# Batch 0's first chain and batch 1's v, regrouped: V spread beside k.z, A in halves, v loaded whole, stores and tails in other places of the queue

## The chip, the cores and the metric

The kernel runs on one core of a Trainium2 chip. The metric is device time in microseconds (us), the median of several executions; lower is better. The chip's engines run beside each other: TensorE (PE, with its weight loads PEld), VectorE (DVE), ScalarE (ACT), GpSimd (POOL) and the queue engine SyncE (SP). DMAs are issued from SP's, POOL's or ACT's queue. Each engine works through its own instructions in the program's order and waits at semaphores for the others.

## The reference, cut to what matters

Eight batches, eight heads, a sequence of 576, a head width of 64. A cosine-weighted linear attention feeds a mixer with a low-rank product over the sequence and an MLP over the channels:

```python
# q, k, v: (8, 8, 576, 64)
phi(x) = concat([relu(x) * cos(theta), relu(x) * sin(theta)])   # theta = pi/2 * pos / 576
kv  = einsum('bhsf,bhsd->bhfd', phi(k), v);  z = phi(k).sum(over s)
x   = einsum('bhsf,bhfd->bhsd', phi(q), kv) / (einsum('bhsf,bhf->bhs', phi(q), z) + 1e-6)
x   -> (8, 576, 512)                                # heads side by side
u   = x + ((x^T @ U) @ V)^T                         # U: 576x32, V: 32x576
out = u + relu(u @ w_ch1) @ w_ch2                   # w_ch1: 512x2048, w_ch2: 2048x512
```

## The kernel before

A sequence of 576 is cut into four chunks of 128 rows (c = 0 to 3) and a tail of 64 (c = 4). The rows lie so that a partition holds consecutive rows of the sequence: a load of q, k or v has an "odd" DMA (`load_odd`, four rows for every odd partition) and an "even" one (`load_even`, five rows for every even partition, the fifth being the tail). From batch 2 on the tail has a DMA of its own (`load_tail`) beside the two of `load_main`. The staging buffers `qst`, `kst` and `vst` exist once each; a batch's load waits until the batch before has been read out of them.

The program is an order written out by hand (manual schedule). Each engine's instructions stand in the order in which the Python code emits them. Buffers come from pools; a PSUM tile takes the next buffer of its tag (X: one pair of banks; T: one; o: two; g: three) and waits until the last user of that buffer is done.

**The head (batch 0).** PE runs warm-up matmuls on zeros (`keep_warm`) while q, k and v of batch 0 land. DVE and ACT make phi(q) (`q_prep`), PE transposes it, DVE and ACT copy it out; then comes phi(k) (`k_prep`), and for each chunk eight one-column matmuls add up z (L842), with one warm-up matmul after each chunk. `cast_uv` on POOL prepares U and V. Then `first_chain(0)`: v is cast in blocks, `kv_unit` makes kv for four heads at a time (heads 0 to 3, then 4 to 7), `den_mm` and `recip` make the reciprocal of the denominator, `xh_mm` makes x of four heads of one chunk, and `xh_norm` (L728, DVE) multiplies it by the reciprocal. `spread_v` (L223, L226) spreads V over the partitions, in the middle of the second group of x; ACT casts it. `a_mm` makes A = x^T U for the columns 0 to 255, later for 256 to 511; `open_mm` transposes x into a PSUM tile `uT_ps` for one quarter d of the channels, `uTd_mm` adds V^T A to it, and `uTd_evac` casts it to `uT`.

**The mixer.** `g1_main(b, j)` multiplies uT by column block j (of 16) of w_ch1: four matmuls of 512 columns, then a relu on ACT (`hid`). w_ch1 and w_ch2 are loaded by POOL in four DMAs each (`w1_load(n)` holds j = 4n to 4n+3). `g2_part(pr, cc, part)` multiplies hid by a quarter of w_ch2's rows; after the fourth part DVE adds u (`o_sb`), and a DMA stores it. Batches go in pairs pr = 0 to 3; cc = 0 to 3 are the first batch's chunks, cc = 4 is both tails, and 5 to 8 are the second's chunks.

**Slots.** The main part is a list of slots: one `g1_main`, one `g1_tail` or one `g2_part` each, four matmuls of 512 columns (0.86 us) as a rule. Pair 0 has the slots 0 to 15 (g1 of batch 0), 16 to 31 (the early g2 parts of cc 0 to 3), 32 to 47 (g1 of batch 1), 48 to 51 (tails), 52 to 71 (the rest of g2); pair 1 begins at slot 72 with 32 slots of g1, 4 of tails and then 36 of g2. After slot i come the thunks put at i: attention steps of the next batch, loads, DMA transposes. For batch 1 these are `q_prep` and `qtr_unit` (slots 0 to 5), `k_prep` (6, 7, 9, 10, 12), `v_prep` of heads 0 to 3 at 11 and of heads 4 to 7 at 13 (both on DVE), `kv_unit` of heads 0 to 3 at 14 and of 4 to 7 at 15, x from 16 on. Batches 2 to 7 follow `attention_plan`.

```python
for i in range(2):
    at(11 + 2 * i, lambda c=c, i=i: v_prep(1, 4 * i, 4 * i + 4, (c,), (V_,)))
for hg in range(2):
    at(14 + hg, lambda hg=hg: kv_unit(1, hg, "T", 1))
```

Batch 1's v is loaded by four DMAs, odd and even rows of heads 0 to 3 and then of heads 4 to 7. In pair 0 the stores of cc 0 to 4 and 8 go out on POOL as soon as they are ready, those of cc 5 and 6 on SP at slot 65 (`late`), that of cc 7 on SP at once.

## Time and profile before

| | |
|---|---|
| three runs, median (lowest to highest) | 309.15 us (309.09 to 309.82) |
| profiled execution | 309.09 us |
| its span (first to last instruction) | 307.3 us |
| PE busy | 300.0 us (98%) in 2304 matmuls |
| DVE, ACT, POOL busy | 149.2, 139.5, 51.6 us |
| granted TensorE clock, mean | 0.997 |
| HBM read and written | 36.86 and 9.44 MB |

What lies between the span and the execution's time (309.09 - 307.3 = 1.8 us) is the start and the end of the program around its instructions. In the page a row names line, engine, operation, out<-in, its shape and count, and then busy time, mean duration in ns, and the idle time before it with what ended it. Timeline rows have start, length, engine and line; a bracket at the end tells how long the engine had been idle and what it waited for. Consecutive matmuls overlap in these rows: one of 512 columns lasts 379 ns, but the next begins 216 ns after it. A DMA's row (SPq) is its issue alone; its landing is told apart.

### The profile page before, as it was taken

What the parts mean: (1) busy time and instruction counts of PE and PEld (TensorE: products, weight loads), DVE (VectorE), ACT (ScalarE), POOL (GpSimd) and SP (SyncE); (2) the same over time, 40 slices, a digit from 0 to 9 for tenths busy, and PEclk for the clock granted to TensorE, in tenths of its full rate; (3) what the DMA queues carried; (4) which work ended last, traced back from release to release, by engine and by line L of the source; (5) the groups of instructions that cost most, each with busy time, mean ns of one, the idle gap of its engine ahead of it and who ended that gap; (6) DMA issues with size and microseconds to landing.
All of it is one profiled execution on the core that took longest, in us unless ns stands there. A gap on an engine that the chain in (4) does not pass through costs nothing.

```text
span 307.3 us, 5726 instructions
## 1 busy us (share of the span) xinstructions
PE 300.0 (98%) x2304; PEld 157.3 (51%) x2329; DVE 149.2 (49%) x354; ACT 139.5 (45%) x237; POOL 51.6 (17%) x91
## 2 busy tenths in 40 slices
PE   8989999999999999999999999999999999999995
PEld 3676464448445444664455444574455444474443
DVE  4988565873876592166336591146327510001111
ACT  2935921265860566589100466579200366630000
POOL 8411200350120016004221400004221000000000
PEclk9999999999999999999999999999999999999998
DMA  6999999999999969992989579922971140001221
GB/s 213 352 260 255 245 194 233 229 329 221 293 215 203 300 147 264 243 250 78 212 213 344 164 124 218 275 64 79 182 161 46 58 85 0 0 2 68 78 95 68
DMA packets 90445, 54.26 MB, mean 177 GB/s; under 512 B 58484, under 2 KB 87444, under 8 KB 90420
## 3 DMA queue, kind: packets, MB, share of 16 engines
q1 hardware_dynamic: 83956, 43.20, 60.0%
q0 software_dynamic: 6320, 10.64, 14.1%
q8 instruction: 18, 0.29, 0.4%
q10 hardware_dynamic: 144, 0.07, 0.1%
q14 instruction: 7, 0.06, 0.1%
HBM read 36.86 MB, written 9.44 MB: 151 GB/s over the span
## 4 chain that ended last, share of the span: by engine, by line
PE 94%; DMA 2%; DVE 1%; issue 1%; ACT 0%; ACTq 0%; DVEq 0%
PE o_ps L585 40%; PE g_ps L531 36%; PE gt_ps L551 5%; PE kv_ps L299 3%; PE x_ps L390 2%; DMA qst<-in_q_dram 2%; PE va_ps L435 2%; PE t_ps L328 1%; PE a_ps L415 1%; PE t_ps L316 1%; PE w_ps L193 1%; PE z_ps L842 0%; PE va_ps L438 0%; PE x_ps L904 0%; DVE x_bf L728 0%
## 5 line engine op out<-in xcount | busy, mean ns | idle before, releaser
L540 ACT ACTIVATE hid<-g_ps 128x512 bf16<-128x512 f32 x128 | 76.1, 598 | 106.9 <-PE g_ps L531 106.8
L585 PE MATMUL o_ps<-w_bf,hid 128*128 128x512 bf16 (+2 forms) x509 | 117.4, 372 | 0.9
L531 PE MATMUL g_ps<-uT,w_bf 128*128 128x512 bf16 x512 | 116.8, 379 | 0.0
L531 PEld LDWEIGHTS <-w_bf 128*128 128x128 bf16 x512 | 48.7, 98 | 56.9 <-issue 1.7
L585 PEld LDWEIGHTS <-hid 128*128 128x128 bf16 x528 | 48.5, 98 | 51.9 <-issue 1.1
L595 DVE TENSOR_TENSOR o_sb<-u_bf,o_ps 128x512 f32<-128x512 bf16 (+2 forms) x33 | 22.1, 669 | 57.0 <-PE o_ps L585 55.9
L608 POOL DMA_DIRECT2D out_dram<-o_sb x21 | 13.2, 630 | 125.5 <-DVE o_sb L595 56.3
L110 POOL CAST v_ext<-vst 128x512 bf16<-128x512 f32 (+1 forms) x26 | 20.6, 815 | 27.5 <-PE g_ps L531 14.8
L110 DVE CAST kv<-kv_ps 128x260 bf16<-128x260 f32 (+1 forms) x15 | 6.4, 429 | 37.2 <-PE kv_ps L299 37.2
L442 DVE TENSOR_TENSOR u_bf<-x_bf,va_ps 128x512 bf16<-128x512 bf16 x24 | 16.5, 687 | 10.1 <-PE va_ps L435 10.1
L363 DVE TENSOR_SCALAR rec<-x_ps 128x8 f32<-128x8 f32 (+2 forms) x39 | 6.3, 162 | 20.1 <-PE x_ps L390 19.4
L551 PE MATMUL gt_ps<-uT_tl,w_bf 128*128 128x128 bf16 x256 | 15.9, 219 | 0.0
L400 DVE TENSOR_TENSOR x_bf<-x_ps,rec 128x512 bf16<-128x512 f32 x22 | 15.2, 691 | 0.8
L551 PEld LDWEIGHTS <-w_bf 128*128 128x128 bf16 x256 | 14.7, 98 | 0.9
L585 PE MATMUL o_ps<-w_bf,hid_tl 128*128 128x512 bf16 x61 | 14.6, 379 | 0.2
L193 PE MATMUL w_ps<-zero 128*128 128x512 bf16 x36 | 11.9, 445 | 1.3 <-DVE zero L119 1.2
L299 PEld LDWEIGHTS <-k_p 128*128 128x128 bf16 x256 | 11.2, 97 | 3.2
L558 ACT ACTIVATE hid_tl<-gt_ps 128x512 bf16<-128x512 f32 x16 | 9.6, 597 | 6.6 <-PE gt_ps L551 6.6
L258 ACT ACTIVATE k_p<-kst,sinw 128x512 bf16<-128x512 f32 x17 | 11.9, 714 | 0.0
L299 PE MATMUL kv_ps<-v_ext,k_p 128*128 128x65 bf16 (+1 forms) x256 | 11.8, 193 | 0.0
L260 DVE TENSOR_SCALAR q_p<-qst,cosw 128x512 bf16<-128x512 f32 x21 | 9.8, 479 | 3.1 <-DMA qst<-in_q_dram 3.1
L390 PEld LDWEIGHTS <-q_pT 128*128 128x128 bf16 x176 | 8.5, 98 | 4.7
(137 smaller groups left out, 245.9 us busy)
## 6 DMA issues: line engine op xcount, KB each, us to landing
qst<-in_q_dram SPq DMA_DIRECT2D x14, 512.0 KB, 5.8
kst<-in_k_dram SPq DMA_DIRECT2D x14, 512.0 KB, 7.5
vst<-in_v_dram SPq DMA_DIRECT2D x12, 512.0 KB, 8.4
out_dram<-o_sb POOLq DMA_DIRECT2D x21, 256.0 KB, 4.7
w_bf<-in_moe_w_ch_dram POOLq DMA_DIRECT2D x8, 512.0 KB, 12.7
out_dram<-o_sb SPq DMA_DIRECT2D x10, 256.0 KB, 2.4
qst<-in_q_dram SPq DMA_DIRECT2D x2, 640.0 KB, 6.5
kst<-in_k_dram SPq DMA_DIRECT2D x2, 640.0 KB
```

The costliest lines, as they stand in the source:

```text
L110: eng.tensor_copy(out=o, in_=i)
L193: nc.tensor.matmul(out=w_ps, lhsT=zero[:, 0:P], rhs=zero, start=True, stop=True)
L299: nc.tensor.matmul(out=acc[:, i, :], lhsT=k_of(b, c, h), rhs=v_tl[:, h, 0:n] if c == 4 and b < 2 else vx[:, c, h, 0:n], start=(c == 0), st ...
L390: nc.tensor.matmul(out=acc[:, g, i * E : i * E + E], lhsT=qT_of(b, c, h), rhs=kv_sb[b][:, h, :], start=True, stop=True,)
L400: nc.vector.tensor_tensor(out=x_of(b, c, rows).rearrange("p (g i d) -> p g i d", g=2, d=D), in0=view[:, :, :, 0:D], in1=rec[rows].unsqueez ...
L442: nc.vector.tensor_tensor(out=u_bf[b][:, c, :] if c < 4 else u_tl[b // 2], in0=x_of(b, c), in1=va, op=ALU.add,)
L531: nc.tensor.matmul(out=g_ps.rearrange("p (c t) -> p c t", c=4), lhsT=w1_bf[:, d, j * P : j * P + P], rhs=uT[b][:, :, d, :], start=(d == 0) ...
L540: nc.scalar.activation(out=hid[b][:, j, :], in_=g_ps, func=AF.Relu, bias=0.0, scale=1.0)
L551: nc.tensor.matmul(out=g_ps[:, jj, :], lhsT=w1_bf[:, d, j * P : j * P + P], rhs=uT_tl[pr][:, d, :], start=(d == 0), stop=(d == 3),)
L585: nc.tensor.matmul(out=o[:, cols], lhsT=lhs[:, j, c * P : c * P + P], rhs=w2_bf[:, j, cols], start=(j == 0), stop=(j == NJ - 1),)
L595: nc.vector.tensor_tensor(out=o_sb[:, cols], in0=u[:, cols], in1=o[:, cols], op=ALU.add)
L608: eng.dma_start(out=out[b].rearrange("(m k) n -> m k n", k=9)[:, c : c + 6 : 5, cols], in_=o_sb[:, cols],)
```

## The change

- The odd rows of batch 0's q are issued from ACT's queue, not SP's.
- V's spread: its two matmuls stand after chunk 2 of the z loop, in two tiles of tag g, and replace the warm-up matmul there. The other warm-up matmuls of that loop write the second bank of z's own tile, and the last one a tile of tag o. ACT's casts of V stand before kv's.
- First chain: x of heads 0 to 3 of one chunk (ORD[3]) is normalised by four ACT instructions in place of one on DVE. x of heads 4 to 7 uses the three g buffers and the pair X. A's first half, the four quarters of uT and the first g matmuls are in a new order: quarters 0 and 1 of uT in tags T and o, 2 and 3 in X and T; the first three j get their matmuls for d = 0 together (`g_half`), then those for d = 1.
- Batch 1's v is loaded by two DMAs, odd and even rows of all heads.
- Pair 0's stores of cc 1 to 4 go to SP at slot 92; `o_sb` has eight buffers in place of four. cc 5 to 8 and cc 0 stay as they were.
- Batch 2's loads: q's main rows at slot 15, its tail at 26, then k's and v's tail and main rows at 26. Its `q_prep` takes the tail last.

```diff
-    load_odd(qst, q, 0)
+    load_odd(qst, q, 0, eng=A_)
...
-    def spread_v(eng):
-        v_ps = ps.tile([P, 2, 512], FP32, tag="X", bufs=1, name="v_ps")
...
+    def spread_v():
+        for cs in (slice(0, 512), slice(512, S)):
+            t = ps.tile([P, 512], FP32, tag="g", bufs=3, name="v_ps")
+            n = cs.stop - cs.start
+            nc.tensor.matmul(
+                out=t[:, 0:n], lhsT=four, rhs=V_nat[:, cs], start=True, stop=True
+            )
+            v_ps.append(t)
+    def spread_evac(eng):
+        cast(eng, V_bf, v_ps[0].rearrange("r (c p) -> r c p", c=4))
+        cast(eng, V_tl, v_ps[1][:, 0:TS])
...
+    def g_half(b, d, js):
+        for j in js:
+            if d == 0:
+                g_open[b, j] = ps.tile([P, 512], FP32, tag="g", bufs=3, name="g_ps")
+            nc.tensor.matmul(
+                out=g_open[b, j].rearrange("p (c t) -> p c t", c=4),
+                lhsT=w1_bf[:, d, j * P : j * P + P],
+                rhs=uT[b][:, :, d, :],
+                start=(d == 0),
+                stop=False,
+            )
...
-        o_sb = pool.tile([P, DM], FP32, tag="o_sb", bufs=4, name="o_sb")
+        o_sb = pool.tile([P, DM], FP32, tag="o_sb", bufs=8, name="o_sb")
...
+        if pr == 0 and 0 < cc < 8:
+            eng = nc.sync
...
-        if pr == 0 and 5 <= cc < 8:
-            eng = nc.sync
-            if cc < 7:
-                late.append(store)
-                return
+        if pr == 0 and 0 < cc < 7:
+            late.setdefault(92 if cc < 5 else 65, []).append(store)
+            return
         store()
...
-            put(f_at + n, q_prep, c, (q_eng, q_eng))
+            put(f_at + ((n - 1) % 5 if b == 2 else n), q_prep, c, (q_eng, q_eng))
...
         v_prep(b, 4, 8, (4,), (A_,))
+        spread_evac(A_)
...
         x0.append(xh_mm(b, ORD[4], 0, *O2))
+        for i in range(4):
+            nc.scalar.activation(
+                out=x_of(b, ORD[3])[:, i * D : i * D + D], in_=x0[3][:, i, :],
+                func=AF.Copy, bias=0.0, scale=rec[0][:, ORD[3], i : i + 1],
+            )
+        xh_norm(b, ORD[2], 0, rec[0], x0[2])
+        recip(rec[1], d[1])
+        xh_norm(b, ORD[4], 0, rec[0], x0[4])
...
-        x1 = [xh_mm(b, c, 4, *t) for c, t in zip(ORD, (T1, G3))]
-        spread_v(A_)
-        x1 += [xh_mm(b, c, 4, *t) for c, t in zip(ORD[2:], (G3, G3, O2))]
-        for n in range(5):
-            xh_norm(b, ORD[n], 4, rec[1], x1[n])
+        x1 = [xh_mm(b, c, 4, *G3) for c in ORD[0:3]]
+        x34 = ps.tile([P, 2, 512], FP32, tag="X", bufs=1, name="x34_ps")
+        for i in range(2):
+            x1.append(x34[:, i, 0:256].rearrange("p (i d) -> p i d", d=D))
+            xh_mm(b, ORD[3 + i], 4, acc=x1[-1])
...
+        for i, (tag, bufs) in enumerate((T1, O2)):
+            uT_ps[b, i] = ps.tile([P, 4, P], FP32, tag=tag, bufs=bufs, name="uT_ps")
+            open_mm(b, i, uT_ps[b, i], range(4))
         for i in range(2):
-            open_mm(b, i, t[i], range(4))
-        uTd_mm(b, 0)
+            uTd_mm(b, i)
         uTd_evac(b, 0, A_)
-        uTd_mm(b, 1)
+        for n in range(5):
+            xh_norm(b, ORD[n], 4, rec[1], x1[n])
         uTd_evac(b, 1, V_)
         a_mm(b, a_ps, 256, 512, range(5))
         cast(A_, A_of(b)[:, 256:512], a_ps[:, 256:512])
...
+        js = range(3)
+        g_half(b, 0, js)
+        for i in (2, 3):
+            uTd_mm(b, i)
+        g_half(b, 1, js)
+        uTd_evac(b, 2, V_)
+        uTd_evac(b, 3, A_)
...
-    for h0 in (0, 4):
-        load_odd(vst, v, 1, h0, h0 + 4)
-        load_even(vst, v, 1, h0, h0 + 4)
+    load_odd(vst, v, 1)
+    load_even(vst, v, 1)
...
-        if n == 1:
-            put(15, lambda: load_tail(kst, k, 2))
-            put(26, lambda: load_main(kst, k, 2))
-        else:
-            put((15, 0, 26)[n], t)
+        if n == 0:
+            put(15, lambda: load_main(qst, q, 2))
+            put(26, lambda: load_tail(qst, q, 2))
+        else:
+            put(26, t)
```

More of the change, by code (lines that the diff above doesn't have):

```diff
@@ L71, in load_even, with load_odd @@
         )
-    def load_odd(dst, src, b, h0=0, h1=H):
-        nc.sync.dma_start(
+    def load_odd(dst, src, b, h0=0, h1=H, eng=nc.sync):
+        eng.dma_start(
             out=dst[1:P:2, h0:h1, 0:4].rearrange("m h c d -> m h (c d)"),
@@ L219, in cast_uv @@
             cast(G_, U_bf[tail(i), 4 + i, :], stU[tail(i), 4, :])
-    def spread_v(eng):
-        v_ps = ps.tile([P, 2, 512], FP32, tag="X", bufs=1, name="v_ps")
-        nc.tensor.matmul(
-            out=v_ps[:, 0, :], lhsT=four, rhs=V_nat[:, 0:512], start=True, stop=True
-        )
-        nc.tensor.matmul(
-            out=v_ps[:, 1, 0:TS], lhsT=four, rhs=V_nat[:, 512:S], start=True, stop=True
-        )
-        cast(eng, V_bf, v_ps[:, 0, :].rearrange("r (c p) -> r c p", c=4))
-        cast(eng, V_tl, v_ps[:, 1, 0:TS])
+    v_ps = []
+    def spread_v():
[9 more added lines that the diff above has]
+        cast(eng, V_tl, v_ps[1][:, 0:TS])
     k_p, q_p, q_pT, kv_sb, x_bf = {}, {}, {}, {}, {}
@@ L563 @@
     o_ps = {}
-    late = []
+    late = {}
     def g2_part(pr, cc, part):
@@ L598, in g2_part @@
         eng = nc.gpsimd if pr < NPAIR - 1 else nc.scalar if part == 3 and last else nc.sync
-        if cc == 4:
-            for i in range(2):
-                eng.dma_start(
-                    out=out[2 * pr + i].rearrange("(m k) n -> m k n", k=9)[:, 4, :],
-                    in_=o_sb[i * TS : i * TS + TS, :],
-                )
-            return
-        def store():
+        if pr == 0 and 0 < cc < 8:
+            eng = nc.sync
+        def store():
+            if cc == 4:
+                for i in range(2):
+                    eng.dma_start(
+                        out=out[2 * pr + i].rearrange("(m k) n -> m k n", k=9)[:, 4, :],
+                        in_=o_sb[i * TS : i * TS + TS, :],
+                    )
+                return
             eng.dma_start(
@@ L611, in store @@
             )
-        if pr == 0 and 5 <= cc < 8:
-            eng = nc.sync
-            if cc < 7:
-                late.append(store)
-                return
+        if pr == 0 and 0 < cc < 7:
+            late.setdefault(92 if cc < 5 else 65, []).append(store)
+            return
         store()
@@ L714, in den_mm, with xh_mm @@
                 )
-    def xh_mm(b, c, h0, tag, bufs):
-        acc = ps.tile([P, 4, D], FP32, tag=tag, bufs=bufs, name="xh_ps")
+    def xh_mm(b, c, h0, tag=None, bufs=None, acc=None):
+        if acc is None:
+            acc = ps.tile([P, 4, D], FP32, tag=tag, bufs=bufs, name="xh_ps")
         for h in range(h0, h0 + 4):
@@ L788, in first_chain @@
         x0.append(xh_mm(b, ORD[4], 0, *O2))
+        for i in range(4):
+            nc.scalar.activation(
+                out=x_of(b, ORD[3])[:, i * D : i * D + D], in_=x0[3][:, i, :],
+                func=AF.Copy, bias=0.0, scale=rec[0][:, ORD[3], i : i + 1],
+            )
+        xh_norm(b, ORD[2], 0, rec[0], x0[2])
+        recip(rec[1], d[1])
+        xh_norm(b, ORD[4], 0, rec[0], x0[4])
         for _ in range(2):
@@ L792, in first_chain @@
             )
-        for n in range(2, 5):
-            xh_norm(b, ORD[n], 0, rec[0], x0[n])
-            if n == 3:
-                recip(rec[1], d[1])
-        x1 = [xh_mm(b, c, 4, *t) for c, t in zip(ORD, (T1, G3))]
-        spread_v(A_)
-        x1 += [xh_mm(b, c, 4, *t) for c, t in zip(ORD[2:], (G3, G3, O2))]
-        for n in range(5):
-            xh_norm(b, ORD[n], 4, rec[1], x1[n])
+        x1 = [xh_mm(b, c, 4, *G3) for c in ORD[0:3]]
+        x34 = ps.tile([P, 2, 512], FP32, tag="X", bufs=1, name="x34_ps")
+        for i in range(2):
+            x1.append(x34[:, i, 0:256].rearrange("p (i d) -> p i d", d=D))
+            xh_mm(b, ORD[3 + i], 4, acc=x1[-1])
         uT_alloc(b)
-        u03 = ps.tile([P, 2, 512], FP32, tag="X", bufs=1, name="u03")
-        t = [u03[:, i, :].rearrange("p (c t) -> p c t", c=4) for i in range(2)]
         a_ps = ps.tile([P, DM], FP32, tag="o", bufs=2, name="a_ps")
@@ L807, in first_chain @@
         cast(A_, A_of(b)[:, 0:256], a_ps[:, 0:256])
-        for tag, bufs in (T1, O2):
-            t.insert(-1, ps.tile([P, 4, P], FP32, tag=tag, bufs=bufs, name="uT_ps"))
-        for i in range(4):
-            uT_ps[b, i] = t[i]
+        for i, (tag, bufs) in enumerate((T1, O2)):
+            uT_ps[b, i] = ps.tile([P, 4, P], FP32, tag=tag, bufs=bufs, name="uT_ps")
+            open_mm(b, i, uT_ps[b, i], range(4))
         for i in range(2):
-            open_mm(b, i, t[i], range(4))
-        uTd_mm(b, 0)
+            uTd_mm(b, i)
         uTd_evac(b, 0, A_)
-        uTd_mm(b, 1)
+        for n in range(5):
+            xh_norm(b, ORD[n], 4, rec[1], x1[n])
         uTd_evac(b, 1, V_)
@@ L819, in first_chain @@
         cast(A_, A_of(b)[:, 256:512], a_ps[:, 256:512])
-        open_mm(b, 3, t[3], range(4))
-        open_mm(b, 2, t[2], range(4))
+        u2 = ps.tile([P, 2, 512], FP32, tag="X", bufs=1, name="u2")
+        for i in (2, 3):
+            uT_ps[b, i] = (
+                u2[:, 0, :].rearrange("p (c t) -> p c t", c=4) if i == 2
+                else ps.tile([P, 4, P], FP32, tag="T", bufs=1, name="uT_ps")
+            )
+            open_mm(b, i, uT_ps[b, i], range(4))
+        js = range(3)
+        g_half(b, 0, js)
+        for i in (2, 3):
+            uTd_mm(b, i)
+        g_half(b, 1, js)
+        uTd_evac(b, 2, V_)
+        uTd_evac(b, 3, A_)
     FEATS = [(V_, V_ if c == 3 else A_) for c in TL]
@@ L836 @@
     keep_warm(5, "X", 1)
+    cast_uv()
     z_all = ps.tile([P, 2, 512], FP32, tag="X", bufs=1, name="z_ps")
@@ L845 @@
             )
-        keep_warm(1, *G3)
-    cast_uv()
+        if c == 2:
+            spread_v()
+        elif c == 4:
+            keep_warm(1, *O2)
+        else:
+            nc.tensor.matmul(
+                out=z_all[:, 1, :], lhsT=zero[:, 0:P], rhs=zero, start=True, stop=True
+            )
     G_.tensor_copy(out=mark, in_=vst[0:TS, 3, 4, 0:1])
@@ L862 @@
         w2_load(n)
-    g1_main(0, 0, True)
-    uTd_close(0, 2, V_)
-    uTd_close(0, 3, A_)
-    g1_main(0, 1, True)
-    g1_main(0, 2, True)
     q_prep(1, 4, (V_, A_))
@@ L990 @@
             put(at, t)
-    put(65, lambda: [store() for store in late])
+    for n in (65, 92):
+        put(n, lambda n=n: [store() for store in late[n]])
     for i, s in enumerate(slots):
```

## The prediction

> **What bounds the kernel now.** I read the chain of waits first (page, part 4).

> ```profile
> PE 94%; DMA 2%; DVE 1%; issue 1%; ACT 0%; ACTq 0%; DVEq 0%
> ```

> TensorE is the chain. The windows view tells where it has slack (us, then busy time of PE, PEld, DVE, ACT, POOL, clock, DMA share, GB/s).

> ```profile
> 16.20:22.90 6.70, 5.92 (x142) 4.67 (x139) 5.42 (x16) 2.35 (x6) 0.31 (x1) 1.00 1.18 247
> ...
> 25.90:39.00 13.10, 13.10 (x102) 7.21 (x100) 9.56 (x26) 10.03 (x19) 3.14 (x5) 1.00 1.18 246
> ```

> From 22.9 us PE has no holes, so only two things can move the end: holes taken out of the head, and new holes put into the full stretch. Each counts one for one. The timeline shows the head's holes (start, length, then the wait in brackets):

> ```profile
> 19.40 0.29 PE L719 MATMUL xh_ps<-kv,q_tlT 128*128 128x64 bf16 x4 [0.46 <-DVE rec L364]
> ...
> 20.20 0.60 ACT L108 ACTIVATE V_bf<-v_ps 128x512 bf16<-128x512 f32 x1 [1.81 <-PE v_ps L226]
> ...
> 22.47 0.38 PE L761 MATMUL u<-ident,x_bf 128*128 128x128 bf16 x4 [0.22 <-ACT uT L108]
> ```

> And DVE's timeline, 14 us later, shows what stands close behind PE: batch 1's v, landing in two halves.

> ```profile
> 33.53 0.30 DVE L110 CAST v_tl<-vst 128x256 bf16<-128x256 f32 x1
> 33.74 0.90 DVE L110 CAST v_ext<-vst 128x256 bf16<-128x256 f32 x4
> 34.54 0.48 DVE L260 TENSOR_SCALAR k_p<-kst,cosw 128x512 bf16<-128x512 f32 x1
> 38.01 0.30 DVE L110 CAST v_tl<-vst 128x256 bf16<-128x256 f32 x1 [2.99 <-DMA vst<-in_v_dram]
> 38.22 0.90 DVE L110 CAST v_ext<-vst 128x256 bf16<-128x256 f32 x4
> ```

> Heads 0 to 3 are cast at 33.53 without a wait. Heads 4 to 7 wait 2.99 us for their DMA (last issue at 20.24, landing 17.7 us later by the vst view: 37.9). PE starts kv of heads 0 to 3 at 38.53 and of heads 4 to 7 at 39.99, when the second casts (end 39.12) are done: today this costs nothing.

> **The change, part by part.** All times are of the profiled execution: 309.09 us, of which 307.3 are span; the median of the three runs, 309.15, is 0.06 above it.

> *q's odd rows on ScalarE's queue.* SP's next load (L68, 1.70) doesn't start when the first ends (0.73 + 0.77 = 1.50), but when qst's memset does (1.19 + 0.48 = 1.67). So it stays at 1.70, and k and v behind it stay. The engines carry the same bytes (352 GB/s from 7.5 to 12.8). Cost 0, bounds -0.2 to +0.2 (the slack of 1.70 over 1.50).

> *V's spread beside k.z.* Two matmuls (19.74 to 20.09, 0.35 us) leave the head for a place where PE pads with warm-up matmuls and waits for DVE and ACT (15.12: PEld waits 0.30). One warm-up of 512 columns goes too, without value there. ACT's two casts (20.20 to 20.91) move to 15.63, where ACT then idles until 18.00 (2.37). V_tl's end at 16.45 is before x's second group needs that bank (16.96): cover 0.5; if it were gone, PE would wait by the excess.

> *First chain.* PE's holes beyond the matmuls' own time: 0.62 at 19.40 (bank T waits for the second reciprocal), 0.23 at 20.96 (bank X waits for V_tl's cast), 0.38 at 22.47 (the bank pair waits for both casts of uT): 1.23. With x's second group in banks g and X, all three go. ACT's four 128x64 normalisations (four took 0.9 at L914) follow kv's cast at 18.39 and end at 19.3; DVE drops one of 0.36. So x of heads 0 to 3 is complete at 19.4 instead of 19.52, and PE reaches A's first half at 19.65 instead of 20.57. Cast (0.38) at 20.4, closing matmuls at 20.5. New holes: 0.1 there; 0.3 before A's second half, as DVE's five norms (0.42 + 4 x 0.36) now end near 21.2; 0.1 before g of j=0 gets its third and fourth matmul (uT 2 and 3, casts of 0.69 and 0.60). Sum: -1.23 - 0.35 + 0.5 = -1.1, bounds -0.7 to -1.2. Stepping through, these g matmuls come at 23.8 instead of 24.64: -0.85. I take -0.85, the lower sum, as DVE's row ends it.

> This gain meets w1 next: the fourth quarter lands 19.5 us after its issue at 15.8, at 35.3, and PE needs it for j=12, now at 38.53 - 3 x 0.863 = 35.94. So at most 0.62 is kept after j=12.

> *Batch 1's v whole.* Two issues of twice the size for four. The second half's landing now holds all casts. Same queue, same bytes, the same neighbours (w1, then w2): I take the landing at 37.9. In DVE's order nothing else moves: v_tl, four v_ext, k_p of c=3, then v of heads 4 to 7. Behind the wait is k_p, and PE's kv of heads 0 to 3 waits for that. From the first cast's start to k_p's end took 34.54 + 0.48 - 33.53 = 1.49; from 38.01 that is 39.50. PE follows DVE's end by 0.05 (kv's cast ended at 16.79, x began at 16.84): 39.55. The matmul that reads k_p's c=3 is the fourth, 38.62 today. **+0.93**, however early PE gets there. The second casts then start at 39.41 (k_p's step is 0.39) and end at 40.5, kv's own cast (0.43) at 40.86; PE reaches heads 4 to 7 at 39.55 + 0.5 + 0.86 = 40.9: no second hole. Without the change PE would have had 39.99: the same +0.93.

> Bounds of the landing: the first half's today (33.5, no hole) and k's pace. k, loaded whole, took from q's landing (17.7, DMA trace) to 29.0, less a quiet 0.9 us, 10.4 us; v's halves took 8.9 after it. At k's pace v lands at 39.3: +2.3. I stay at 37.9, since the second half is its nearest row, queued behind the same bytes.

> *Stores, tails and batch 2's loads.* Four of pair 0's POOL issues go: cc 1 to 3 and, in two, cc 4 are stored from SP at slot 92: 5 x 0.63 = 3.2 us ahead of batch 5's loads (slot 94), which are first read at slot 110, 14 us later. q's and k's tails now stand behind the two uT transposes; k's main loads are issued about 1.3 us later (two issues of 0.65) and land near 62.6 instead of 61.3; five k_preps of 2 x 0.4 end at 66.6, and PE asks at slot 46 (57.22 + 14 x 0.863 = 69.3): cover 2.7. uT of batch 1, with fewer loads ahead, can only come earlier than 56.4, and PE reads it at 57.22. Eight o_sb buffers: slot 108 is the first to reuse one stored at 92. All 0, bounds -0.3 (PE's hole before a_ps at 83) to +0.3.

> Sum: the head's -0.85 runs into +0.93 measured from today's schedule, which replaces it: 309.09 + 0.93 = **310.0 us**.

> **Rivals.**

> *v lands early enough.* What decides is the landing. From it to kv's fourth matmul are 0.09 (37.92 to 38.01) + 1.49 + 0.05 = 1.63: 38.62 - 1.63 = 37.0 is break-even, and 36.4 leaves all that w1 leaves, -0.62: 308.5, not slower. If w1's quarter comes earlier as well, -0.85: 308.2. For it: eleven of the sixteen DMA engines have done their share of the last v load by 35.7, and the last three hold its end to 37.4 to 37.9. Against: those few carry the same bytes after the change. [...] The rows speak against it: whole k was no faster than v in halves.

> *v lands late*, at whole k's pace: 309.09 + 2.3 = 311.4.

> *The hole cools PE.* It would be idle for 1.6 us. At the end of the run the granted clock falls to 0.50 from 305.7, 2.0 us after the last matmul:

> ```profile
> 304.00:305.00 1.00, 0.00 (x0) 0.00 (x0) 0.00 (x0) 0.00 (x0) 0.00 (x0) 1.00 0.40 151
> ...
> 305.70:307.30 1.60, 0.00 (x0) 0.00 (x0) 0.00 (x0) 0.00 (x0) 0.00 (x0) 0.50 0.00 0
> ```

> If 1.6 us sufficed, PE would run at half clock as long as at the start (matmuls 0.43 apart until 5.3, some 4 us): 2 us lost, 312.0. Against: a hole of 0.84 at 18.56 did nothing. [...]

> *The queue part does more than I see* (the hole at 83 goes and v is no hindrance): 308.2.

> **How the numbers follow.** A measurement of this kernel can tell about 0.3%, 0.93 us, from no change; the forecast lies on that line. Forecast (landing 37.4 to 38.4) 0.45, of which 0.27 above the line; late v 0.12; cooled PE 0.08: slower 0.47. Early v or the queue part 0.27, 0.18 of it beyond -0.93 (the head's lower bound -1.2, w1 early): faster 0.18. The rest, landing between 36.4 and 37.4, 0.08, with early v's 0.09 and the forecast's 0.18: same 0.35. Range: 308.2 (early v) to 311.4 (late v); it leaves out the cooled PE and the last tenth of early v.

> **What would show it.** Right: in the new profile DVE's first v cast of batch 1 waits for the vst DMA until about 38, PE's kv of heads 0 to 3 waits for DVE's k_p until 39.5, and PE stands 0.6 to 0.9 us ahead of before at j=8. The holes at 19.40, 20.96 and 22.47 are gone; V_bf's cast stands at 15.6. Wrong: v landing before 37.0, no wait at kv, or j=12 waiting for w1 by more than 0.3. A slower head would not even show in the end, as long as it loses under 0.9.

## The result, and the profile after

| | before | after |
|---|---|---|
| median of 18 runs each (lowest to highest) | 309.11 us (308.85 to 309.82) | 309.76 us (309.35 to 310.69) |
| profiled execution, its span | 309.09, 307.3 us | 309.55, 307.8 us |
| kv's fourth matmul of batch 1 (the one that reads k_p's c=3) | 38.62 us | 39.45 us |
| last matmul of TensorE | 303.43 us | 304.26 us |

The change makes the kernel slower by 0.65 us: ratio 1.0022, 95% interval 1.0015 to 1.0029. The forecast was 310.0. The two lower rows of the table agree to 0.01 (+0.83 and +0.82): from batch 1's kv to the last matmul the two kernels run the same distance, so all of TensorE's loss is made before it. The profiled executions differ by less, 0.46 us, because the stretch from the last matmul to the end of the span is 3.89 us before and 3.52 after. There SyncE waits for the DMAs' semaphores one after another, and four such waits come behind that of the last store before, one after, so that SyncE is through 0.24 us sooner.

The chain of waits (by engine, then by line) now has the loads of batch 1's v in it:

```profile
PE 86%; DMA 9%; ACT 2%; DVE 1%; issue 1%; SPq 0%; ACTq 0%; DVEq 0%
PE o_ps L601 41%; PE g_ps L535 32%; DMA vst<-in_v_dram 7%; PE gt_ps L567 5%; PE kv_ps L303 3%; PE x_ps L394 2%; DMA qst<-in_q_dram 2%; PE va_ps L439 2%; PE a_ps L419 1%; ACT q_p L262 1%; ACT k_p L262 1%; PE va_ps L442 0%; PE x_ps L936 0%; ACT q_pT L108 0%; DVE v_ext L110 0%
```

Before, TensorE met kv without a wait:

```profile
38.53 0.28 PE L299 MATMUL kv_ps<-v_ext,k_p 128*128 128x65 bf16 x4
```

DVE's timeline after, around the landing (start, length, engine, line; the bracket is the idle time ahead and what ended it):

```profile
37.80 0.30 DVE L110 CAST v_tl<-vst 128x256 bf16<-128x256 f32 x1 [4.82 <-DMA vst<-in_v_dram]
38.01 0.90 DVE L110 CAST v_ext<-vst 128x256 bf16<-128x256 f32 x4
38.82 0.48 DVE L264 TENSOR_SCALAR k_p<-kst,cosw 128x512 bf16<-128x512 f32 x1
```

DVE now stands idle for 4.82 us until v's even rows land (37.71). The casts of heads 0 to 3, done at 34.5 before, end at 38.9, and k_p behind them at 39.30. TensorE's timeline shows the answer, first in the head, then at kv:

```profile
18.44 0.38 PE L816 MATMUL d_ps<-zero 128*128 128x512 bf16 x1
19.28 0.38 PE L816 MATMUL d_ps<-zero 128*128 128x512 bf16 x1 [0.46 <-issue]
19.49 0.29 PE L736 MATMUL xh_ps<-kv,q_tlT 128*128 128x64 bf16 x4
```

```profile
38.35 0.59 PE L303 MATMUL kv_ps<-v_ext,k_p 128*128 128x65 bf16 x3 [0.17 <-DVE v_ext L110]
39.45 0.19 PE L303 MATMUL kv_ps<-v_ext,k_p 128*128 128x65 bf16 x1 [0.50 <-DVE k_p L264]
```

In the head the holes at 20.96 and 22.47 are gone, but one stands at 19.28, now with nothing to wait for but "issue": 0.83 from the first zero matmul to the second, of which 0.22 are the first one's own time. Its length is thus 0.62. Past it there is no hole up to kv. The windows view (busy time of PE, PEld, DVE, ACT, POOL, then clock, DMA share, GB/s) gives both stretches:

```profile
19.30:22.90 3.60, 3.60 (x58) 2.35 (x58) 2.43 (x6) 1.25 (x3) 0.00 (x0) 1.00 1.17 247
25.90:37.90 12.00, 12.00 (x81) 6.45 (x80) 6.76 (x15) 8.98 (x17) 3.45 (x5) 1.00 1.18 249
37.90:39.50 1.60, 0.91 (x7) 0.28 (x6) 1.60 (x8) 0.94 (x2) 0.00 (x0) 1.00 1.24 205
```

TensorE came 0.51 us earlier out of the head (first g with all its matmuls, j=0 d=2, at 24.13 against 24.64), kept that to 38.0, and lost it and 0.83 more at kv.

### The profile page after: what moved, and what is told of

It is laid out like the page before. It is cut to its first block, busy times and chain, and to the rows that moved or that the text cites. A ratio compares the mean times of both kernels' runs of the same rounds, so it can differ in the third digit from the quotient of the medians.

```text
span 307.8 us, 5736 instructions
## 1 busy us (share of the span) xinstructions
PE 301.4 (98%) x2328; PEld 157.1 (51%) x2328; DVE 148.8 (48%) x353; ACT 140.2 (46%) x241; POOL 48.7 (16%) x86
## 4 chain that ended last, share of the span: by engine, by line
PE 86%; DMA 9%; ACT 2%; DVE 1%; issue 1%; SPq 0%; ACTq 0%; DVEq 0%
PE o_ps L601 41%; PE g_ps L535 32%; DMA vst<-in_v_dram 7%; PE gt_ps L567 5%; PE kv_ps L303 3%; PE x_ps L394 2%; DMA qst<-in_q_dram 2%; PE va_ps L439 2%; PE a_ps L419 1%; ACT q_p L262 1%; ACT k_p L262 1%; PE va_ps L442 0%; PE x_ps L936 0%; ACT q_pT L108 0%; DVE v_ext L110 0%
## 5 line engine op out<-in xcount | busy, mean ns | idle before, releaser
L601 PE MATMUL o_ps<-w_bf,hid 128*128 128x512 bf16 (+2 forms) x528 | 119.7, 373 | 0.0
L535 PE MATMUL g_ps<-uT,w_bf 128*128 128x512 bf16 x506 | 115.3, 379 | 0.0
L535 PEld LDWEIGHTS <-w_bf 128*128 128x128 bf16 x506 | 48.0, 98 | 56.6 <-issue 1.9
L626 POOL DMA_DIRECT2D out_dram<-o_sb x18 | 11.3, 629 | 126.2 <-DVE o_sb L611 48.6
L110 POOL CAST v_ext<-vst 128x512 bf16<-128x512 f32 (+1 forms) x26 | 20.7, 818 | 43.4 <-DMA vst<-in_v_dram 43.2
L110 DVE CAST kv<-kv_ps 128x260 bf16<-128x260 f32 (+1 forms) x15 | 6.4, 428 | 38.1 <-PE kv_ps L303 38.1
L446 DVE TENSOR_TENSOR u_bf<-x_bf,va_ps 128x512 bf16<-128x512 bf16 x24 | 16.5, 686 | 10.2 <-PE va_ps L439 10.2
L367 DVE TENSOR_SCALAR rec<-x_ps 128x8 f32<-128x8 f32 (+2 forms) x39 | 6.3, 161 | 20.1 <-PE x_ps L394 19.4
L567 PEld LDWEIGHTS <-w_bf 128*128 128x128 bf16 x256 | 14.7, 98 | 0.9
L193 PE MATMUL w_ps<-zero 128*128 128x512 bf16 x33 | 9.9, 434 | 1.2 <-DVE zero L119 1.2
```

The costliest lines, as they stand in the source:

```text
L110: eng.tensor_copy(out=o, in_=i)
L446: nc.vector.tensor_tensor(out=u_bf[b][:, c, :] if c < 4 else u_tl[b // 2], in0=x_of(b, c), in1=va, op=ALU.add,)
L535: nc.tensor.matmul(out=g_ps.rearrange("p (c t) -> p c t", c=4), lhsT=w1_bf[:, d, j * P : j * P + P], rhs=uT[b][:, :, d, :], start=(d == 0) ...
L567: nc.tensor.matmul(out=g_ps[:, jj, :], lhsT=w1_bf[:, d, j * P : j * P + P], rhs=uT_tl[pr][:, d, :], start=(d == 0), stop=(d == 3),)
L601: nc.tensor.matmul(out=o[:, cols], lhsT=lhs[:, j, c * P : c * P + P], rhs=w2_bf[:, j, cols], start=(j == 0), stop=(j == NJ - 1),)
L626: eng.dma_start(out=out[b].rearrange("(m k) n -> m k n", k=9)[:, c : c + 6 : 5, cols], in_=o_sb[:, cols],)
```

## The experiments

The first four kernels tell the two parts apart (A: v whole makes the hole at kv; B: stores and tails) and ask what the hole at 19.28 is (C: TensorE waits for its own instructions; D: it waits for an engine or a bank).

**v in halves again, the rest of the change kept.**

```diff
-    load_odd(vst, v, 1)
-    load_even(vst, v, 1)
+    for h0 in (0, 4):
+        load_odd(vst, v, 1, h0, h0 + 4)
+        load_even(vst, v, 1, h0, h0 + 4)
```

> The changed kernel with batch 1's v in two halves again, nothing else undone. Theory A (v loaded whole makes the hole in PE at kv of heads 0 to 3, and nothing else costs): the hole is gone, the first kv matmul starts 0.5 us earlier than in the kernel before (38.0), all that the head has gained (0.51 at the first completed g) is kept, since w1's last quarter (35.2) is just in time: 308.6, 0.5 below before. Theory B (the loss lies in the stores, tails and loads of the later part): the time stays near 309.8. If w1 binds, 308.5 to 308.9.

Measured: 308.91 us median beside 309.23 for the kernel before on that chip (ratio 0.9998, 0.9978 to 1.0019); profiled 308.88. No wait at kv: its fourth matmul at 38.38. The second half of v landed at 37.87, as late as ever, but only the second casts wait for it:

```profile
37.96 0.30 DVE L110 CAST v_tl<-vst 128x256 bf16<-128x256 f32 x1 [2.96 <-DMA vst<-in_v_dram]
```

So A. The head kept only 0.24 of its gain here (308.6 was expected), because the hole in it was longer, 1.11 us from one zero matmul to the next against 0.83 in the kernel after:

```profile
19.54 0.38 PE L816 MATMUL d_ps<-zero 128*128 128x512 bf16 x1 [0.74 <-issue]
```

**The kernel before, with v whole.** The reverse of the diff above, put into the kernel before.

> The kernel before with batch 1's v loaded by two DMAs, the only edit. Theory A: DVE's first v cast of batch 1 waits until 37.8, k_p of c=3 ends 1.5 us later, PE's fourth kv matmul starts at 39.4 to 39.6 instead of 38.62: +0.8 to +1.0, 310.0, more than the whole change cost, as nothing of it depends on the head. Theory B: no difference from before.

Measured: 310.08 us beside 309.23, ratio 1.0029 (1.0012 to 1.0046). One edit alone gives the whole loss, and at the same instruction:

```profile
39.60 0.19 PE L299 MATMUL kv_ps<-v_ext,k_p 128*128 128x65 bf16 x1 [0.50 <-DVE k_p L260]
```

kv's fourth matmul came 0.98 later than before. B falls: without any store or tail moved the time is as long. The head of this kernel is that of the kernel before, and here both zero matmuls have their records:

```profile
18.52 0.59 PE L790 MATMUL d_ps<-zero 128*128 128x512 bf16 x2
19.18 0.28 PE L719 MATMUL xh_ps<-kv,q_tlT 128*128 128x64 bf16 x4
```

The second one starts at 18.74, so TensorE is free at 18.96, and x of heads 4 to 7 comes 0.23 later.

**k_p ahead of v on DVE.** In the kernel after, batch 1's last k_prep two slots earlier.

```diff
-        at((6, 7, 9, 10, 12)[n], lambda c=c: k_prep(1, c, (V_, A_)))
+        at((6, 7, 9, 10, 10)[n], lambda c=c: k_prep(1, c, (V_, A_)))
```

> The changed kernel (v whole) with k_prep of c=3 at slot 10 instead of 12, so that DVE does it ahead of the casts that wait for v. Theory A with k_p as the last link: PE then waits for v_ext of c=3 alone (ends 38.9): the fourth kv matmul at 39.0 instead of 39.45, 0.4 to 0.5 us less than the changed kernel, 309.3. If the casts or the bank set the hole and k_p does not: no change from the changed kernel, 309.8.

Measured: profiled 309.04, median 309.55 beside 309.23 (ratio 1.0008, 0.9984 to 1.0032). kv's fourth matmul at 38.92, 0.53 earlier than in the kernel after, with v landing as late (37.67). So some 0.5 of the 0.83 is k_p queued behind v's casts, and 0.30 is the casts themselves, which stay. The hole in the head was down to 0.07: q had landed 0.5 later (7.82), and TensorE came to the place that much later.

**Fewer instructions ahead of the hole.** v in halves, and z of chunks 0 to 3 left out (its output lacks them), 56 TensorE instructions fewer.

```diff
-        for h in range(H):
+        for h in range(H if c == 4 else 0):
...
+        if c < 4:
+            nc.tensor.matmul(
+                out=z_all[:, 1, :], lhsT=zero[:, 0:P], rhs=zero, start=True, stop=True
```

> v in halves as in the first run; and z leaves out chunks 0 to 3 (32 one-column matmuls), with one warm-up matmul more per chunk: 28 matmuls, 56 instructions with their weight loads, fewer in PE's stream ahead of the first chain. It tells what the hole in PE at 18.7 to 19.3 is, which the change was to remove and did not. Theory C (PE has run out of fetched instructions: the hole comes after a fixed number of instructions, some 448, and ends when the next fetch is in): the same point of the stream is now reached after A's first half, later than 19.3, so there is no hole, x of heads 4 to 7 starts at 18.9 instead of 19.5, and the first completed g comes 0.4 to 0.6 us earlier than in the first run; the end gains less, since w1's last quarter (35.2) then binds: 308.4. Theory D (PE waits for another engine or for a bank): the hole stands where it stood, between the two zero matmuls, and the time is that of the first run.

Measured: profiled 309.17, median 309.8 beside 309.23. The zero matmuls now follow each other without a gap, and the hole stands 56 instructions further on in the work, in front of uT, where nothing had waited:

```profile
19.70 0.20 PE L771 MATMUL a_ps<-x_tl,U_bf 128*32 128x64 bf16 x4
21.15 0.61 PE L778 MATMUL uT_ps<-ident,x_bf 128*128 128x128 bf16 x8 [1.25 <-issue]
```

Counted in the trace it is the same place: 448 recorded TensorE instructions lie ahead of it here, in the kernel after and in the one with v in halves. That agrees with C. The gain that C promised did not come: the hole got longer. The DMA part of the page lists a queue named instruction, with 18 packets of 16 KB in the whole span (19 in the three kernels below with 132 more TensorE instructions):

```profile
q8 instruction: 18, 0.29, 0.4%
```

The DMA view of 16.5 to 18.5 us of the kernel after holds one of them:

```profile
q8 instruction: 1, 0.02, 3.5%
```

Its start and the moment at which TensorE goes on lie 2.35 to 2.57 us apart in every run with a hole:

| kernel | packet starts | instructions ahead | TensorE goes on | later by |
|---|---|---|---|---|
| before | 16.93 | 446 | 19.40 | 2.47 |
| before, v whole | 16.82 | 448 | 19.18 | 2.36 |
| after | 16.86 | 448 | 19.28 | 2.42 |
| v in halves | 16.98 | 448 | 19.54 | 2.56 |
| k_p ahead of v | 16.77 | 448 | 19.26 | 2.49 |
| fewer instructions | 18.80 | 448 | 21.15 | 2.35 |
| head alone (below) | 16.81 | 448 | 19.22 | 2.41 |
| head alone, 72 more (below) | 16.79 | 446 | 19.36 | 2.57 |

Where 446 stands, two matmuls ahead of the hole have no record though their weight loads have, so it is 448 in every row. In the kernel before one of the two is the second zero matmul. The weight load that follows it stands in PEld's timeline at 18.78, where the matmul must have begun:

```profile
18.78 0.10 PEld L719 LDWEIGHTS <-q_tlT 128*128 128x128 bf16 x1
```

So TensorE was free at 18.99 there, and the hole of the kernel before is 0.41 long and lies behind both zero matmuls. In the kernel after one more matmul stands ahead, and the hole lies one matmul earlier, between the two.

The end of the hole thus follows the packet, and not how early TensorE stands before it. That the packet is what TensorE waits for is an inference from these distances; no trace names it.

**The place moved 132 instructions forward.** The 22 warm-up matmuls at the start in four pieces each, in three kernels: the one with v in halves, the kernel before, the kernel after.

```diff
-    keep_warm(22, "X", 1)
+    keep_warm(22, "X", 1, 4)
```

> The changed kernel with batch 1's v in halves (as e1_v_halves), and the 22 warm-up matmuls of 512 columns at the start each in four pieces of 128 columns: same columns, 66 matmuls and 66 weight loads more ahead of the head, so every later instruction stands 132 further back in PE's stream. Theory C (the hole at 18.7 to 19.5 us is PE waiting for its next block of instructions, at a fixed place in its stream, about 449 seen instructions in): the place comes 132 instructions earlier in the work, at about 317 of the old count, near 16 us, and the block is then asked for near 13 us, well before it is needed, so no hole; the next place is where matmuls are 216 ns apart. The two zero matmuls and x of heads 4 to 7 follow back to back, g of j=0 d=2 at 23.5 (24.40 in e1), at most 0.6 to 0.7 of it kept after j=12 (w1's last quarter lands at 35.2): 308.4 to 308.5 against 308.9 in e1 and 309.1 before. Theory D (the hole is a wait for a bank or an engine): the hole stays, 308.9.

> The kernel before, with only the 22 warm-up matmuls in four pieces each (132 PE instructions more ahead of the head). This tests the step of the prediction that put 0.62 us at 19.40 down to bank T waiting for the second reciprocal. If that is so, the hole stays and the time is 309.1. If it was the instruction fetch, the hole shrinks or goes, x of heads 4 to 7 follows at 18.8 to 18.9, g of j=0 d=2 comes 0.5 to 0.6 earlier (24.1), and the time is 308.5 to 308.6.

> The changed kernel as it is, with v whole, and the 22 warm-up matmuls in four pieces each. The prediction says that v's landing sets kv's fourth matmul however early PE gets there. Then g of j=0 d=2 comes 0.6 earlier (23.5), but kv's fourth matmul stays at 39.4 to 39.6 and the time at 309.6 to 309.8, the same as the changed kernel's. If the head's gain is kept in spite of v, 309.0.

Measured: 309.36, 309.94 and 310.4 us beside 309.28 (ratios 1.0002, 1.0030 and 1.0035, with 0.9988 to 1.0016, 1.0006 to 1.0054 and 1.0006 to 1.0063). The runs of these kernels scatter by 2 to 5 us, so the stages of the trace say more than the medians here; the second and third profiles (312.2 and 313.29) are of executions some 2 and 3 us above their medians. The hole at 19 went in all three; with v in halves the head ran

```profile
19.02 0.59 PE L820 MATMUL d_ps<-zero 128*128 128x512 bf16 x2
19.45 0.29 PE L740 MATMUL xh_ps<-kv,q_tlT 128*128 128x64 bf16 x4
```

without a gap. But the packet now started at 12.0 to 12.5 us, among the packets of batch 0's v, and one of the sixteen DMA engines brought its share of the next loads late: fifteen had theirs of v's odd rows of heads 4 to 7 by 13.36, the last at 15.04, and of the even rows behind them by 14.23 and at 15.99. DVE's cast of that v waits for these, its cast of kv stands behind, and x waits for kv:

```profile
17.30 0.28 PE L740 MATMUL xh_ps<-kv,q_tlT 128*128 128x64 bf16 x4 [0.48 <-DVE kv L110]
```

In the second and third kernel w1's first quarter, which is gated by v, landed at 25.96 and 25.71 (21.92 in the kernel after). In the third TensorE stood still for it:

```profile
25.75 1.27 PE L556 MATMUL g_ps<-uT,w_bf 128*128 128x512 bf16 x3 [3.56 <-DMA w_bf<-in_moe_w_ch_dram]
```

A miss, then: the hole was removed and another was bought. That kernel can't say whether v's landing holds back an earlier TensorE, since TensorE was late.

**The head alone.** v in halves, and stores, tails and batch 2's loads in the order of before.

```diff
-        o_sb = pool.tile([P, DM], FP32, tag="o_sb", bufs=8, name="o_sb")
+        o_sb = pool.tile([P, DM], FP32, tag="o_sb", bufs=4, name="o_sb")
...
-        if n == 0:
-            put(15, lambda: load_main(qst, q, 2))
-            put(26, lambda: load_tail(qst, q, 2))
+        if n == 1:
+            put(15, lambda: load_tail(kst, k, 2))
+            put(26, lambda: load_main(kst, k, 2))
```

> The changed kernel with batch 1's v in halves and the queue part as before (pair 0's stores on POOL and late ones at slot 65, four o_sb buffers, tails and batch 2's loads in the old order): the head's part of the change alone. Theory A with the queue part at nothing: as e1, 308.8 to 308.9 (0.25 to 0.3 below before), kv's fourth matmul at 38.3 to 38.4. Theory B (the queue part carries some of e1's gain): 309.1. If the queue part costs something, 308.6.

Measured: 308.95 us beside 309.28, ratio 0.9991 (0.9978 to 1.0003). kv's fourth matmul at 38.05, 0.57 earlier than before; then a loss of 0.98 on the way to the end, most of it at one place:

```profile
89.84 0.19 PE L303 MATMUL kv_ps<-v_ext,k_p 128*128 128x65 bf16 x1 [0.25 <-POOL v_ext L110]
90.39 0.25 PE L303 MATMUL kv_ps<-v_ext,k_p 128*128 128x65 bf16 x3 [0.36 <-POOL v_ext L110]
```

POOL's cast of this v starts at 89.17, since the load landed at 88.66; it had landed at 87.00 before, and at 85.17 in the kernel with v in halves and the new order, where SP issued it 1.65 earlier (76.77 against 78.42). The old order doesn't explain the late landing: SP issued the load earlier here than in the kernel before (78.42 against 78.85), and fifteen of its sixteen shares were in by 86.37; the last alone came at 88.66. That is one profile of each, and this one (309.31) lies above its median. The medians of the two kernels, each 0.3 below before, show no worth of the queue part, and whether it has one stays open.

**The place moved 72 forward.** Only 12 of the 22 warm-ups in pieces, in the head alone, the kernel before and the kernel after.

```diff
-    keep_warm(22, "X", 1)
+    keep_warm(12, "X", 1, 4)
+    keep_warm(10, "X", 1)
```

> The head's part of the change alone (as e8_head_alone: batch 1's v in halves, stores, tails and batch 2's loads as before), with the first 12 of the 22 warm-up matmuls in four pieces each: 36 matmuls and 36 weight loads more, 72 instructions. With 132 more, the next block of instructions was fetched at 12.0 to 12.5 us, on top of batch 0's v, and one DMA engine's share of v came 1.5 to 2.5 us late. With 72 the fetch should fall at 14 to 15 us, after v has landed (14.4), and be usable near 17, when PE reaches the block's end at about 17.1. Theory C: no hole at 18.6 to 19.5, no wait of kv for v; g of j=0 d=0 starts at 21.9 to 22.2 (w1's first quarter lands at 21.7 to 22.2), kv's fourth matmul of batch 1 at 37.7 to 38.0 (38.04 in e8, 38.62 before): 308.5 to 308.8, which would beat both kernels. If the hole only moves along the stream and stays as long (0.4 to 0.9), 308.9 to 309.1.

> The kernel before with the same 72 more instructions among its warm-ups. Tests again the prediction's step that put the 0.62 us at 19.40 down to bank T and the second reciprocal, this time without disturbing batch 0's v. Instruction fetch: the first x of heads 4 to 7 comes right behind the zero matmuls at 18.8 to 18.9 (19.40 before), g of j=0 d=2 at 24.0 to 24.1 (24.64), time 308.5 to 308.7. Bank T: x stays at 19.2 to 19.4 even when no fetch is near, and the time at 309.1.

> The changed kernel, v whole, with the same 72 more instructions. The prediction says kv's fourth matmul follows v's landing however early PE gets there. So with the hole gone g of j=0 d=2 comes 0.5 to 0.6 earlier (23.5 to 23.6), the hole before kv grows by as much, kv's fourth matmul stays at 39.4 to 39.6, and the time at 309.6 to 309.8. If the head's gain reached the end, 309.1.

Measured: 309.83, 310.86 and 309.65 us beside 309.30 (ratios 1.0023, 1.0044 and 1.0016, with 1.0002 to 1.0044, 1.0019 to 1.0068 and 0.9998 to 1.0034), all three scattered over 2 to 4 us. In the first the packet did not come earlier (16.79), and the hole stood 72 instructions earlier in the work, in the middle of kv of heads 4 to 7:

```profile
17.48 0.25 PE L307 MATMUL kv_ps<-v_ext,k_p 128*128 128x64 bf16 x3
19.36 0.19 PE L307 MATMUL kv_ps<-v_ext,k_p 128*128 128x64 bf16 x1 [1.62 <-issue]
```

In the second it came at 14.66, and there was no hole. With TensorE 0.19 later than in the kernel before, x of heads 4 to 7 starts right behind the two zero matmuls (the second again without a record), at 19.18,

```profile
18.75 0.38 PE L794 MATMUL d_ps<-zero 128*128 128x512 bf16 x1
19.18 0.29 PE L723 MATMUL xh_ps<-kv,q_tlT 128*128 128x64 bf16 x4
```

while DVE's second reciprocal runs from 19.16 to 19.44:

```profile
18.96 0.16 DVE L367 TENSOR_SCALAR rec<-d_ps 128x20 f32<-128x20 f32 x1
19.16 0.28 DVE L368 RECIPROCAL rec<-rec 128x20 f32<-128x20 f32 x1
```

So x doesn't wait for the reciprocal. What reads bank T is the addition ahead of it (L367), which ends here at 19.12, too close to x to tell it from the zero matmuls. The kernel before with v whole tells them apart: there the addition ended at 18.89 and x still started at 19.18; in the kernel before it ended at 18.93, and x started at 19.40. Bank T was free in both while the hole lasted. kv came 0.20 earlier than before; 0.59 were lost later (0.2 of it to uT's transposes at 57), so the time was not better. In the third batch 0's q was late (TensorE's first transpose at 9.62 against 8.16) and no hole showed; v landed at 36.6 there, kv's fourth matmul was at 39.10 without a wait, and the run tells nothing on its question.

No version beats the kernel before by more than its interval. The two with v in halves and the instruction count unchanged come nearest, 0.3 us below it by their medians.

## Why the prediction was right, point by point

*v whole, +0.93.* Right in mechanism, and measured at +0.83. The landing was 37.71, not 37.9 (37.86 in the kernel before with v whole, so this is scatter between runs); from the first cast to k_p's end it took 1.50 as worked out; TensorE then followed k_p's end by 0.15, not 0.05. -0.21, +0.01 and +0.10 give the difference. The second casts ended at 40.31 (said: 40.5), kv of heads 4 to 7 began at 40.82 (40.9), with no second hole. That the loss replaces the head's gain instead of adding to it is seen in the kernel before with v whole: +0.98 without any faster head, against +0.83 with one. The rest between the two is the landing, 37.86 against 37.71.

*From +0.93 to 310.0.* The sum took everything behind kv as unchanged. That holds up to the last matmul (+0.82), but not behind it: the end of the program is 0.37 shorter, for which the prediction has no term. The profiled execution was thus 309.55, and of what is missing from 310.0 most lies there, and 0.10 in kv.

*The landing stays at 37.9.* Right for this change: whole or in halves, the last piece of v came between 37.67 and 37.95 in the seven kernels whose packet started at 16.8 to 17.0. Both rivals fall, the early v and the one at whole k's pace. The longer load landed no earlier (37.71 and 37.86 whole, 37.87 in halves). But the landing isn't fixed: with v whole it came at 36.59 and 34.73 in the kernels after with 72 and 132 more instructions, whose loads of batch 0 came late.

*The head, -0.85.* Wrong in one step, and measured at -0.51. The step that failed is "0.62 at 19.40 (bank T waits for the second reciprocal)", one of the three holes that were all to go. It was 0.41, since the second zero matmul had run unrecorded; it wasn't bank T, which was free at 18.93; and after the change it was 0.62. The other two went, V's spread left the head (V_bf's cast at 15.41), and from x of heads 4 to 7 to j=0 d=2 the head got shorter by 0.60 (5.24 to 4.64), without the new holes of 0.5 that were allowed for. But the first hole stayed, and its end, 19.28, lies 2.42 behind the start of a packet of the queue named instruction, beside 2.35 to 2.57 in the other kernels with a hole. TensorE came to the zero matmuls 0.12 earlier and stood 0.21 longer: with the 0.60 that is the -0.51. The row of before named DVE's reciprocal as what ended the wait: that name is inferred from the last semaphore, and was wrong. The sign "0.6 to 0.9 us ahead of before at j=8" wasn't met either. That none of this shows in the time is no merit of the forecast of the head: v's landing hid it, as the sum said it would hide any gain.

*w1's last quarter.* It landed at 35.19; TensorE was 0.5 ahead and reached it at about 35.4. It never bound. (From its own 35.94 and 35.3 the room was 0.64, not 0.62.)

*q's odd rows: 0.* q landed at 7.28 against 7.41, but at 7.19 to 7.82 over the kernels with this edit and undisturbed loads: no effect to be told from scatter.

*Stores, tails, batch 2's loads: 0.* Right for this kernel: TensorE has no new hole after kv. What the prediction left out is that the cover depends on how early TensorE comes: in the head alone, 0.57 earlier, one late share of batch 3's v, landing 1.66 later than before, cost most of 1 us at 90.

*The cooled TensorE.* Fell: the granted clock is 1.00 throughout the stretch of kv (37.9 to 39.5). The 2.0 us that the rival took from the end of the run are no measure of what is needed: there the clock fell 2.0 us after the last matmul before, 3.6 after the change and 4.9 with v in halves. The last section has the two falls within the work.

On 0.3%: the loss is 0.22%. It lies below what the text called tellable, and 18 runs a side tell it all the same.

## What to carry to other kernels

When loads are merged, look at what the consuming engine has queued behind the first use of the part that used to land early: here DVE's k_p behind v's casts turned a landing 4 us later into a wait of TensorE, though the last bytes came no later. Look at the weight loads before you size a hole: a matmul without a record can hide in it, as the one at 18.78 did. A hole that no engine's work explains is tested by shifting the instruction stream: here it kept its instruction count (448) and not its place in the work, and the edit to that place did not remove it. And a gain in the head is worth only as much as the next deadline leaves, so look for the waits that come within its size first, on every engine.

## What the runs showed of the hardware

A load came late beside a packet: in the three runs with the packet at 12.0 to 12.5 one share of v came 1.4 to 2.2 us behind the other fifteen, and so did those of the loads behind it; in the ten other runs no share of batch 0's v came more than 0.6 behind. Everything that waited for that load waited for it. That the packet delayed it is the author's inference, and a late share alone proves no packet: that of batch 3's v in the head alone came 2.3 us behind, and packets lie within this load's flight in kernels without a late share too.

The clock fell twice within the work. In the kernel after with 132 more instructions TensorE had stood for 3.56 us, and 0.24 after it went on at 25.75 the clock fell to 0.50, for 3.4 us:

```profile
26.00:29.00 3.00, 3.00 (x9) 1.08 (x8) 1.51 (x3) 1.08 (x2) 2.67 (x5) 0.50 1.16 259
```

In the kernel before with 132 more instructions it fell too, at 17.75, again for 3.4 us, and there TensorE had been busy for most of the 3.4 us before, with no more than 0.88 from one matmul's start to the next:

```profile
14.30:17.70 3.40, 2.51 (x67) 1.93 (x64) 1.69 (x5) 1.83 (x5) 2.41 (x4) 1.00 1.08 355
17.80:21.10 3.30, 3.17 (x62) 2.89 (x62) 2.45 (x10) 0.39 (x1) 0.78 (x2) 0.50 1.12 317
```

So TensorE had stood still for 3.56 us ahead of the one fall and for less than 0.88 ahead of the other. The 3.41 us up to the falls hold matmuls of 1024 and 2852 columns together, as recorded. In the kernels before and after the clock was 1.00 from 5.3 to 305.6, and any 3.41 us between 5.3 and 300 hold 3380 columns or more, those around the hole of 0.66 us that the change makes at kv 4250 or more. What the clock goes by was not shown.
